# Loading the first rows of wq in four interleaved sets, from two issuing queues

## The chip, the cores and the metric

The kernel runs on one core of a Trainium2 chip. The metric is the device time of one execution in microseconds (us), the median of several runs. A profile of one execution comes with it; its span, from the first to the last instruction, is about 2 us shorter than the device time.

The engines are named as the profile names them: PE (TensorE; PEld is its weight load), DVE (VectorE), ACT (ScalarE), POOL (GpSimd) and SP (SyncE, which here only issues loads). SP and ACT can both issue loads; "SPq" and "ACTq" in the profile are their issuing instructions. The loads themselves are carried out by 16 DMA engines.

## What is computed

One decode step: of the output's rows there is a single one (batch 1, sequence 1, D = 640). It is a block of attention over a sliding window of 4096 cached keys, with 32 heads of 192 columns, and a gated MLP, each behind a layer norm and with a residual:

```python
def _A_ref(x, k_cache, v_cache, wq, wo):
    B, Sq, D = x.shape                       # 1, 1, 640
    Hq, Dh = (32, 192)
    W = min(4096, max(256, Sk // 4))         # 4096 of 32768 cached rows
    q = (x @ wq).reshape(B, Sq, Hq, Dh)      # wq: 640 x 6144, bf16
    k = k_cache[:, :, Sk - W:, :]
    v = v_cache[:, :, Sk - W:, :]
    scores = einsum('bhqd,bhkd->bhqk', q, k) * Dh ** (-0.5)
    o = einsum('bhqk,bhkd->bhqd', softmax(scores), v)
    return o.reshape(B, Sq, Hq * Dh) @ wo    # wo: 6144 x 640
...
x = A_x
h = x + _A_ref(_layernorm(x), A_k_cache, A_v_cache, A_wq, A_wo)
h2 = h + _B_ref(_layernorm(h), B_w_in, B_w_sp, B_b_sp, B_w_out)
```

The keys and the values of the window are 50 MB each, wq and wo 7.9 MB each, w_in and w_out together 3 MB: about 119 MB in all, each byte of it used once.

## The kernel before

A helper records a load on SP's queue. The views of the tensors in memory decide which rows make one contiguous run:

```python
def load(out, in_):
    eng = nc.sync
    eng.add_instruction(mybir.InstDMACopy(
        name=nc.get_next_instruction_name(), mode="Copy", queue="qSPDynamicHW",
        ins=eng.lower_ap_dma(in_, for_custom_bir_dma=True),
        outs=eng.lower_ap_dma(out, for_custom_bir_dma=True)))
...
wq_v = A_wq.rearrange("(c p i) n -> c p (i n)", c=DC, i=4)
...
kvp = ctx.enter_context(tc.tile_pool(name="kv", bufs=KVB))      # KVB = 6
```

wq has five chunks (DC = 5) of 128 rows of 6144 elements. `wq_v[c]` shows a chunk as 32 runs of four rows each (49,152 bytes), which go to 128 partitions, a row to each. Two chunks share a buffer of the kv pool, which wq, the keys and the values use in turn:

```python
def dma_wq(i):
    t = kvp.tile([P, KVE], BF16, tag="kv", name="wq_t")
    for c in range(2 * i, min(2 * i + 2, DC)):
        load(t[:, (c % 2) * HD:(c % 2 + 1) * HD], wq_v[c])
    tiles[("wq", i)] = t
...
plan = [("kv", lambda i=i: dma_wq(i)) for i in range(NWQ)]      # wq first: three buffers
for t_ in range(2):
    plan.append(("kv", lambda t=t_: dma_pair("k", A_k_cache, t)))
...                                                             # then k and v tiles of 3 MB in turn, wo, w_in, w_out
```

Loads are issued as far ahead as buffers are free: at the start that is all of wq and three tiles of keys. Everything else comes after the first call of `issue()`, in this order:

```python
issue()
warm = const.tile([P, 1], F32)
nc.vector.memset(warm[:], 0.0)
nc.scalar.activation(out=warm[:], in_=warm[:], func=ACT.Exp)
nc.scalar.dma_start(out=x_row[:], in_=A_x[0])
...                                       # two more small loads by ACT, constants on DVE and POOL
xc_ps = bank()                            # L241: x to a column form on PE, then the layer norm -> xn2
...
for gq in range(0, NQ, 4):                # the projection to q: 6 sums of 10 matmuls
    for w0 in range(0, 2 * Dh, P):
        psv = sc_bank()[:].rearrange("p (q w) -> p q w", q=4)
        for c in range(DC):
            wc = wq_sb[c // 2][:, (c % 2) * HD:(c % 2 + 1) * HD].rearrange("p (q a w) -> p q a w", q=NQ, a=2)
            for a in range(2):
                nc.tensor.matmul(psv, lhsT=xn2[:, c, a, :], rhs=wc[:, gq:gq + 4, a, w0:w0 + P],     # L264
                                 start=(c == 0 and a == 0), stop=(c == DC - 1 and a == 1))
        nc.scalar.activation(out=q2f[:, gq:gq + 4, w0:w0 + P], in_=psv, func=ACT.Copy, scale=scale / 16)
free("kv", NWQ)                           # the three wq buffers go to v and k tiles
```

Each of the six sums runs over all five chunks. There are two buffers of PSUM for them. After the projection DVE multiplies each tile of keys by its rows of q (L316), PE and others sum the products, and the values and wo follow tile by tile. The last loads are the second half of the last rows of wo (L478 uses them), w_in and w_out for the MLP.

Of the kernel before, what the change touches and what calls it, by code (L numbers as in the profile page):

```python
# [16 lines left out]
def kernel(  # L17
# [14 lines left out]
    nc = tc.nc  # L32
# [6 lines left out]
    DC = D // P  # L39
    HD = H * Dh  # L40
# [12 lines left out]

    NE16 = 32

    def load(out, in_):
        eng = nc.sync
        eng.add_instruction(mybir.InstDMACopy(  # L58
            name=nc.get_next_instruction_name(), mode="Copy", queue="qSPDynamicHW",
            ins=eng.lower_ap_dma(in_, for_custom_bir_dma=True),  # L60
            outs=eng.lower_ap_dma(out, for_custom_bir_dma=True)))

# [8 lines left out]
    win_v = B_w_in.rearrange("(c p) f -> p c f", p=P)  # L71
    wout_v = B_w_out.rearrange("(c e i) n -> c e (i n)", c=FHC, e=NE16)
    wq_v = A_wq.rearrange("(c p i) n -> c p (i n)", c=DC, i=4)
    LAST = (0, J // 2, 3 * J // 4, 7 * J // 8, J)

    KVB = 6
# [13 lines left out]
    def bank():  # L90
        return psum.tile([P, 512], F32, tag="sm", name="sm_ps", bufs=3)
# [9 lines left out]
    def dma_wq(i):  # L101
        t = kvp.tile([P, KVE], BF16, tag="kv", name="wq_t")
        for c in range(2 * i, min(2 * i + 2, DC)):
            load(t[:, (c % 2) * HD:(c % 2 + 1) * HD], wq_v[c])
        tiles[("wq", i)] = t

    def dma_pair(kind, cache, t_):
        t = kvp.tile([P, KVE], BF16, tag="kv", name=kind + "_t")
        cuts = (0, J) if t_ < NP - 1 else LAST if kind == "v" else (0, J // 2, J)
        for a, b in zip(cuts, cuts[1:]):  # L110
            load(t[:, None, a * Dh:b * Dh], pair_keys(cache, t_, a, b))
        tiles[(kind, t_)] = t

    def dma_wo(q):
        t = wop.tile([P, RQ * D], BF16, tag="wo", name="wo_t")
        if q < NQ - 1:
            load(t[:], wo_v[q])
        else:
            rows_v = A_wo.rearrange("(q p i) n -> q p (i n)", q=NQ, p=P)[q]
            for a in range(0, RQ, RQ // 2):  # L120
                load(t[:, a * D:(a + RQ // 2) * D], rows_v[:, a * D:(a + RQ // 2) * D])
        tiles[("wo", q)] = t

    plan = [("kv", lambda i=i: dma_wq(i)) for i in range(NWQ)]
    for t_ in range(2):
        plan.append(("kv", lambda t=t_: dma_pair("k", A_k_cache, t)))
# [269 lines left out]
    def values(t, vt, lo, hi):  # L396
        E = E_bufs[t % NE]
        pv = pv_tiles[t % 2]
        if t == NP - 1:
            for j in range(lo, hi):  # L400
                p0 = 32 * (j % 4)
                nc.tensor.matmul(pv[p0:p0 + 2, 0:Dh], lhsT=E[:, j, :], rhs=vt[:, j * Dh:(j + 1) * Dh],
                                 start=(j < 4), stop=(j >= J - 4))
            return
        v4 = vt[:].rearrange("p (j r i) -> p j r i", r=32, i=RQ)
        for j in range(lo, hi, 8):
            g = j // 8
            for p0, j0, n, i0 in ((0, j, 4, 0), (32, j + 4, 4, 0), (64 + 32 * (g % 2), j, 8, 4)):
                ni = 16 // n
                first = j == 0 if n == 4 else g < 2  # L410
                last = j == J - 8 if n == 4 else g >= J // 8 - 2
                nc.tensor.matmul(pv[p0:p0 + 2 * n, :].rearrange("p (k r i) -> p k r i", k=n, r=32),  # L412
                                 lhsT=E[:, j0:j0 + n, :].rearrange("p j a -> p (j a)"),
                                 rhs=v4[:, j0:j0 + n, :, i0:i0 + ni], start=first, stop=last)

    def scaled(t):
        q, b = divmod(t, 2)
        if b == 0:
            obq[q] = small.tile([P, RQ, 2, 2, 32], BF16, tag="ob", name="ob", bufs=2)
        ob = obq[q][:, :, 0, b, :]  # L420
        pv = pv_tiles[t % 2]
        if t == NP - 1:
            pv1 = pv[:, 0:Dh].rearrange("p (r i) -> p i r", i=RQ)
            R2 = RQ // 2
            for k_ in range(2):
                o_last.append(small.tile([P, R2, 32], BF16, tag=f"ol{k_}", name=f"ol{k_}", bufs=1))
            nc.vector.tensor_copy(out=o_last[0][:], in_=pv1[:, 0:R2])
            nc.scalar.copy(out=o_last[1][:], in_=pv1[:, R2:])
            return
        o1 = small.tile([P, 8, 64], F32, tag="o1", name="o1", bufs=1)  # L430
        nc.vector.tensor_tensor(out=o1[:], in0=pv[:].rearrange("p (k w) -> p k w", k=8),
                                in1=m8[:, :, None].to_broadcast([P, 8, 64]), op=ALU.mult)
        flat = o1[:].rearrange("p k w -> p (k w)")
        for n, i0 in ((4, 0), (8, 4)):
            ni = 16 // n
            with nc.allow_low_precision(reason="one nonzero term"):
                nc.vector.tensor_reduce(out=ob[:, i0:i0 + ni], in_=flat.rearrange("p (k r i) -> p i r k", k=n, i=ni),  # L437
                                        axis=AX.X, op=ALU.add)

    def columns(oT, q, b):  # L440
        for i in range(RQ):
            lhsT = obq[q][:, i, 0, 0, :] if b == 0 else o_last[i // 3][:, i % 3, :]
            s_ = sel[i // 4] if b == 0 else sel_1
            for a in range(2):
                p0 = 64 * a + 32 * b
                nc.tensor.matmul(oT[p0:p0 + 32, i:i + 1], lhsT=lhsT, rhs=s_[:, a:a + 1], start=True, stop=True)
# [36 lines left out]
    def fold(rows_sb):  # L483
        n = CUT[1] // P
        for c in range(n):
            w = 2 if c + n < DC else 1
            nc.tensor.matmul(attn_ps[:, c:c + n * (w - 1) + 1:n], lhsT=rows_sb[:, c * P:(c + 1) * P], rhs=halfsel[:, 0:w],
                             start=(c == 0), stop=False)
# [71 lines left out]
    vt = tiles.pop(("v", NP - 1))  # L560
    values(NP - 1, vt, 0, LAST[-3])
    fold(rows_sb)
    values(NP - 1, vt, LAST[-3], LAST[-2])
    oT = bank()
    columns(oT, NQ - 1, 0)
    values(NP - 1, vt, LAST[-2], J)
    scaled(NP - 1)
# [90 lines left out]
```

## Time and profile before

| what | value |
|---|---|
| device time, median of 3 runs | 286.56 us (286.56 to 286.75) |
| span of the profiled execution | 284.7 us |
| busiest engine | DVE, 218.4 us |
| bytes on SP's load queue | 119.35 MB |
| wq loads | 5 of 1536 KB each, median 11.2 us from issue to landing |
| first wq issue by SP; issue of x_row by ACT | 0.74 us; 0.91 us |
| first and last start of a projection matmul | 9.8 us; 34.9 us |

How to read such a profile: the busy shares say which engine works most, but not which of them sets the end. For that one looks at the stages one by one, at the load queues beside the engines, and at the chain of waits that ended last, followed back from the last instruction. The records of the DMA packets, from which the loads' share comes, give the start, length and size of every single transfer on the 16 DMA engines. Times in the views are in us from the start of the span; "L264" is a line of the kernel.

### The profile page before, as it was taken

What the parts mean: (1) busy time and instruction counts of PE and PEld (TensorE: products, weight loads), DVE (VectorE), ACT (ScalarE), POOL (GpSimd) and SP (SyncE); (2) the same over time, 40 slices, a digit from 0 to 9 for tenths busy, and PEclk for the clock granted to TensorE, in tenths of its full rate; (3) what the DMA queues carried; (4) which work ended last, traced back from release to release, by engine and by line L of the source; (5) the groups of instructions that cost most, each with busy time, mean ns of one, the idle gap of its engine ahead of it and who ended that gap; (6) DMA issues with size and microseconds to landing.
All of it is one profiled execution on the core that took longest, in us unless ns stands there. A gap on an engine that the chain in (4) does not pass through costs nothing.

```text
span 284.7 us, 3101 instructions
## 1 busy us (share of the span) xinstructions
PE 167.1 (59%) x1110; PEld 65.3 (23%) x1110; DVE 218.4 (77%) x288; ACT 75.2 (26%) x380; POOL 2.3 (1%) x10
## 2 busy tenths in 40 slices
PE   0329935773755377725852585536971767764774
PEld 0103412221211022211220121112320222321463
DVE  7300099889999999998499999996699949995443
ACT  2001247413274431122344440143101010202301
POOL 3000000000000000000000000000000000000000
PEclk9999979796598557955799558955797797999785
DMA  8999999999998999999999999999999999999993
GB/s 332 435 435 408 435 429 402 444 463 435 435 435 382 435 442 443 427 464 424 414 442 421 443 428 439 407 457 428 410 435 456 442 442 383 435 435 425 401 406 141
DMA packets 5404, 119.53 MB, mean 420 GB/s; under 512 B 973, under 2 KB 2254, under 8 KB 2830
## 3 DMA queue, kind: packets, MB, share of 16 engines
q1 hardware_dynamic: 5384, 119.35, 97.8%
q8 instruction: 8, 0.13, 0.2%
q14 instruction: 6, 0.05, 0.0%
q10 hardware_dynamic: 6, 0.00, 0.0%
HBM read 119.34 MB, written 0.00 MB: 419 GB/s over the span
## 4 chain that ended last, share of the span: by engine, by line
DMA 42%; DVE 41%; PE 13%; issue 2%; SPq 1%; ACT 0%; DVEq 0%; ACTq 0%
DVE k_t L316 22%; DMA k_t<-in_A_k_cache_dram 21%; DMA v_t<-in_A_v_cache_dram 9%; DMA wq_t<-in_A_wq_dram 7%; DMA wo_t<-in_A_wo_dram 5%; PE sc_ps L264 5%; DVE S L309 5%; DVE ob L437 4%; DVE S L330 4%; PE sc_ps L323 3%; PE pv_174 L412 1%; PE attn_ps L473 1%; SPq L58 1%; PE sm_ps L340 1%; DVE gm L342 1%
## 5 line engine op out<-in xcount | busy, mean ns | idle before, releaser
L316 DVE TENSOR_TENSOR k_t<-k_t,q_205 128x6144 bf16<-128x6144 bf16 x32 | 107.1, 3351 | 13.1 <-DMA k_t<-in_A_k_cache_dram 13.1
L323 PE MATMUL sc_ps<-k_t,ident_bf 128*128 128x512 bf16 x282 | 87.1, 468 | 50.6 <-DVE k_t L316 50.6
L306 ACT ACTIVATE k_t<-k_t 128x192 bf16<-128x192 bf16 x144 | 49.9, 347 | 32.8 <-DVE k_t L316 32.8
L323 PEld LDWEIGHTS <-ident_bf 128*128 128x128 bf16 x282 | 30.6, 113 | 98.3 <-issue 63.9
L306 ACT ACTIVATION_READ_ACCUMULATOR k_t<-k_t 128x1 f32 x144 | 26.8, 186 | 0.0
L309 DVE TENSOR_REDUCE S<-k_t 128x16 f32<-128x3072 bf16 x8 | 26.8, 3345 | 0.0
L264 PE MATMUL sc_ps<-wq_t,xn_126 128*128 128x512 bf16 x60 | 17.4, 449 | 10.4 <-DMA wq_t<-in_A_wq_dram 8.1
L330 DVE TENSOR_REDUCE S<-sc_ps 128x16 f32<-128x512 f32 (+1 forms) x32 | 21.8, 682 | 0.5 <-PE sc_ps L323 0.5
L273 DVE TENSOR_SCALAR sp_f<-sm_ps 128x1 f32<-128x1 f32 x3 | 0.3, 153 | 25.3 <-PE sm_ps L270 25.3
L359 ACT ACTIVATE E_125<-S,bias 128x64 bf16<-128x64 f32 x10 | 3.5, 360 | 48.1 <-DVE bias L349 48.1
L359 ACT ACTIVATE E_123<-S,bias 128x64 bf16<-128x64 f32 x12 | 4.2, 360 | 41.9 <-DVE bias L349 41.9
L359 ACT ACTIVATE E_124<-S,bias 128x64 bf16<-128x64 f32 x10 | 3.5, 361 | 37.9 <-DVE bias L349 37.9
L266 ACT ACTIVATE q_205<-sc_ps 128x512 bf16<-128x512 f32 x6 | 3.6, 597 | 30.1 <-PE sc_ps L264 30.1
L264 PEld LDWEIGHTS <-xn_126 128*128 128x128 bf16 x60 | 6.5, 109 | 20.9 <-issue 13.6
L412 PE MATMUL pv_174<-v_t,E_124 128*8 128x512 bf16 (+1 forms) x72 | 8.9, 521 | 2.0 <-DMA v_t<-in_A_v_cache_dram 2.0
L342 DVE TENSOR_REDUCE gm<-sm_ps 2x1 f32<-2x128 f32 x16 | 4.5, 278 | 7.1 <-PE sm_ps L340 7.1
L412 PE MATMUL pv_172<-v_t,E_125 128*8 128x512 bf16 (+1 forms) x72 | 7.5, 472 | 3.1 <-DMA v_t<-in_A_v_cache_dram 3.1
L412 PE MATMUL pv_174<-v_t,E_123 128*8 128x512 bf16 (+1 forms) x48 | 5.8, 521 | 1.0 <-DMA v_t<-in_A_v_cache_dram 1.0
L412 PE MATMUL pv_172<-v_t,E_123 128*8 128x512 bf16 (+1 forms) x72 | 6.2, 424 | 0.0
L412 PE MATMUL pv_174<-v_t,E_125 128*8 128x512 bf16 (+1 forms) x48 | 5.0, 474 | 1.6 <-DMA v_t<-in_A_v_cache_dram 1.6
L412 PEld LDWEIGHTS <-E_125 128*8 128x8 bf16 (+1 forms) x120 | 3.5, 87 | 9.3 <-issue 7.2
L412 PEld LDWEIGHTS <-E_124 128*8 128x8 bf16 (+1 forms) x120 | 3.6, 89 | 8.3 <-issue 6.4
(237 smaller groups left out, 148.3 us busy)
## 6 DMA issues: line engine op xcount, KB each, us to landing
k_t<-in_A_k_cache_dram SPq DMA_DIRECT2D x15, 3072.0 KB, 29.8
v_t<-in_A_v_cache_dram SPq DMA_DIRECT2D x15, 3072.0 KB, 29.6
wq_t<-in_A_wq_dram SPq DMA_DIRECT2D x5, 1536.0 KB, 11.2
wo_t<-in_A_wo_dram SPq DMA_DIRECT2D x7, 960.0 KB, 19.9
k_t<-in_A_k_cache_dram SPq DMA_DIRECT2D x2, 1536.0 KB
v_t<-in_A_v_cache_dram SPq DMA_DIRECT2D x1, 1536.0 KB
w_in_sb<-in_B_w_in_dram SPq DMA_DIRECT2D x2, 576.0 KB, 14.6
wo_t<-in_A_wo_dram SPq DMA_DIRECT2D x2, 480.0 KB, 13.8
```

What stands on the lines that cost most here:

```text
L58: eng.add_instruction(mybir.InstDMACopy(name=nc.get_next_instruction_name(), mode="Copy", queue="qSPDynamicHW", ins=eng.lower_ap_dma(in_, ...
L264: nc.tensor.matmul(psv, lhsT=xn2[:, c, a, :], rhs=wc[:, gq:gq + 4, a, w0:w0 + P], start=(c == 0 and a == 0), stop=(c == DC - 1 and a == 1))
L266: nc.scalar.activation(out=q2f[:, gq:gq + 4, w0:w0 + P], in_=psv, func=ACT.Copy, scale=scale / 16)
L306: nc.scalar.activation(out=k3[:, j, :], in_=k3[:, j, :], func=ACT.Copy, accum_out=S[:, j:j + 1])
L309: nc.vector.tensor_reduce(out=st[t]["S"][:, J - JS:J], in_=products(t)[:, J - JS:J, :], axis=AX.X, op=ALU.add)
L316: nc.vector.tensor_tensor(out=kc, in0=kc, in1=q2[:, t:t + 1, :].to_broadcast([P, JC, Dh]), op=ALU.mult)
L323: nc.tensor.matmul(psv, lhsT=ident_bf[:], rhs=products(t)[:, j0:j1, n * g:(n + 1) * g], start=(n == 0), stop=(n == Dh // g - 1))
L330: nc.vector.tensor_reduce(out=S[:, j0:j1], in_=st[t]["ps"][ch], axis=AX.X, op=ALU.add)
L342: nc.vector.tensor_reduce(out=gm[:], in_=mT[0:2, 0:P], axis=AX.X, op=ALU.max)
L359: nc.scalar.activation(out=E[:, :, a], in_=S[:], func=ACT.Exp, bias=bias[:, a:a + 1], accum_out=zq[q][:, a, b:b + 1])
L412: nc.tensor.matmul(pv[p0:p0 + 2 * n, :].rearrange("p (k r i) -> p k r i", k=n, r=32), lhsT=E[:, j0:j0 + n, :].rearrange("p j a -> p (j a)" ...
L437: nc.vector.tensor_reduce(out=ob[:, i0:i0 + ni], in_=flat.rearrange("p (k r i) -> p i r k", k=n, i=ni), axis=AX.X, op=ALU.add)
```

## The change

The change cuts the loads of the first four wq chunks into sets of interleaved rows: four sets of every fourth row for chunks 0 and 1, two sets of every second row for chunks 2 and 3. Chunk 4 stays as it was. A row is now a run of its own (12,288 bytes). Of chunk 0, sets 1 and 3 are issued from ACT's queue and sets 0 and 2 from SP's, so that two queues have work at the start. Its purpose is to have the first rows under way sooner: each of the first loads is smaller and two of them can be issued at the same time. The same bytes go to the same partitions as before, and nothing else in the program is changed.

```diff
-    def load(out, in_):
-        eng = nc.sync
+    def load(out, in_, eng=nc.sync):
         eng.add_instruction(mybir.InstDMACopy(
-            name=nc.get_next_instruction_name(), mode="Copy", queue="qSPDynamicHW",
+            name=nc.get_next_instruction_name(), mode="Copy", queue="qSPDynamicHW" if eng is nc.sync else "qActDynamicHW",
             ins=eng.lower_ap_dma(in_, for_custom_bir_dma=True),
             outs=eng.lower_ap_dma(out, for_custom_bir_dma=True)))
...
     wq_v = A_wq.rearrange("(c p i) n -> c p (i n)", c=DC, i=4)
+    wq_rows = A_wq.rearrange("(c p) n -> c p n", c=DC)
+    WQ_PARTS = (4, 4, 2, 2, 1)
...
         for c in range(2 * i, min(2 * i + 2, DC)):
-            load(t[:, (c % 2) * HD:(c % 2 + 1) * HD], wq_v[c])
+            n = WQ_PARTS[c]
+            for j in range(n):
+                dst = t[j::n, (c % 2) * HD:(c % 2 + 1) * HD]
+                load(dst, wq_rows[c, j::n] if n > 1 else wq_v[c], nc.scalar if c == 0 and j % 2 else nc.sync)
         tiles[("wq", i)] = t
```

In the call of `issue()` the two loads on ACT's queue stand ahead of the activation that warms up ACT and of the load of x_row.

## The prediction

> **What bounds the kernel now.** I read the page's shares first, then the load by stage, then the start of the timeline, then the waits, the chain of waits and the packet records of the trace.
>
> ```profile
> span 284.7 us, 3101 instructions
> PE 167.1 (59%) x1110; PEld 65.3 (23%) x1110; DVE 218.4 (77%) x288; ACT 75.2 (26%) x380; POOL 2.3 (1%) x10
> ...
> q1 hardware_dynamic: 5384, 119.35, 97.8%
> ```
>
> The busiest engine, DVE, works 77% of the span; the SP load queue (q1) keeps the 16 DMA engines busy for 97.8%. The table by stage says where the other 2.2% are (columns: stretch, length, busy us of each engine, clock, DMA share, GB/s):
>
> ```profile
> 0.00:2.00 2.00, 0.00 (x0) 0.00 (x0) 0.77 (x6) 1.27 (x1) 1.33 (x10) 1.00 0.00 1
> 2.00:22.00 20.00, 5.00 (x16) 1.78 (x17) 6.75 (x48) 0.22 (x2) 0.95 (x1) 1.00 1.03 433
> 22.00:100.00 78.00, 49.38 (x225) 18.10 (x224) 61.38 (x56) 32.38 (x167) 0.00 (x0) 0.83 1.00 432
> 100.00:180.00 80.00, 47.95 (x283) 16.56 (x284) 71.76 (x73) 24.33 (x134) 0.00 (x0) 0.72 1.00 431
> 180.00:260.00 80.00, 49.60 (x311) 18.74 (x311) 67.02 (x75) 11.78 (x60) 0.00 (x0) 0.83 1.00 432
> ...
> 281.00:285.00 4.00, 0.70 (x24) 0.43 (x12) 0.32 (x1) 0.00 (x0) 0.00 (x0) 0.50 0.00 0
> ```
>
> Nothing moves for 2 us, then 431 to 433 GB/s without a hole until the end, then a tail of nearly 4 us without loads. The packet records agree: data run from 2.07 to 280.95 us, and a packet of 49,152 B takes 1.815 us, so 16 engines give 16 x 49,152 / 1.815 us = 433 GB/s. The run is one long load stream with a fixed head and tail. Its end reaches the output through the last wo rows, as the chain of waits says:
>
> ```profile
> 260.22 13.82 DMA wo_t<-in_A_wo_dram
> 274.08 0.54 PE attn_ps L478 x15
> ```
>
> From 274.08 to 284.7 us there are 10.6 us of short dependent steps that the change doesn't touch. So a change in the start of the stream, or in its total work, moves the end by as much; a change of any engine's work in the first 35 us moves nothing unless it starves the stream.
>
> The place that the change touches is this (start, us, what; in brackets the idle time before):
>
> ```profile
> 0.74 3.15 SPq L58 DMA_DIRECT2D wq_t<-in_A_wq_dram  x5
> ...
> 0.91 0.50 ACTq L155 DMA_DIRECT2D x_row<-in_A_x_dram  x1
> ...
> 9.76 1.03 PE L264 MATMUL sc_ps<-wq_t,xn_126 128*128 128x512 bf16 x2 [2.25 <-DVE xn_126 L251]
> ...
> 11.03 1.01 PE L264 MATMUL sc_ps<-wq_t,xn_126 128*128 128x512 bf16 x2 [0.24 <-DMA wq_t<-in_A_wq_dram]
> ...
> 21.95 4.27 PE L264 MATMUL sc_ps<-wq_t,xn_126 128*128 128x512 bf16 x10 [2.60 <-DMA wq_t<-in_A_wq_dram]
> ```
>
> Five issues take 0.55 to 0.63 us each while one chunk of wq (1.57 MB) takes 3.63 us to move, so issuing is far ahead of moving. The first matmuls wait for xn2, not for the first rows. The fifth chunk lands at 21.95, and only then do 52 of the 60 matmuls run (13.3 us): earlier first rows let TensorE begin earlier and wait longer. Even this projection's end is not the bound: the v tile that follows it is issued at 34.02, with the third k tile still moving until about 2.4 + 17.3 MB / 433 GB/s = 42 us.
>
> [...]
>
> **The change part by part.**
>
> *Work of the stream.* Packets are as long as the source's contiguous run. A chunk before is 32 runs of four rows (49,152 B), two per engine. In chunks 0 to 3 a run becomes one row of 12,288 B, eight per engine. The kernel before has 64 packets of that size, for a part of the last v tile: 0.460 us each. One chunk goes from 2 x 1.815 = 3.63 to 8 x 0.460 = 3.68 us, plus some 3 ns between packets: +0.07 us. Four chunks: **+0.27 us**. Chunk 4 keeps its form. Loads go from 5 to 13, and each ends with a small record that costs an engine about 15 ns: 8 x 15 = **+0.12 us**. Sum +0.39 us, on every engine, all on the path.
>
> *Start of the stream.* Before, ten engines begin their first packet at 2.07 to 2.16 us, the other six at 2.32 to 2.90, and these first packets take 2.06 to 2.68 us in place of 1.815. The slowest engine begins at 2.66 and ends at 5.23, as if it had begun at full speed at 3.41. The engines that began early end from 4.45 on, as if begun at 2.64 to 3.03. All engines move the same bytes, so the lag of the last lasts: the ends of first packets are 0.8 us apart, and the ends of the last data at 280 us too. Two first issues side by side[...] should let the late six begin nearer to the others. If the slowest then does as the early ones did, the gain is 3.41 - 3.03 = 0.4 to 3.41 - 2.64 = 0.8 us. How far it goes I can't read from a trace; I choose **-0.55 us**. The first packet itself can hardly come earlier: the four-row store at the end, far smaller, also takes 1.23 us from issue to first packet (282.10 to 283.33), against 1.33 for wq.
>
> *Issue.* SP issues 11 parts, 11 x 0.6 = 6.6 us in place of 3.15; a part of 0.39 MB keeps the engines busy for 0.92 us, more than its 0.6 us of issue. No hole from that.
>
> *x_row.* Its load stands behind two issues of ACT (1.1 us) [...] I expect it near 6.2 in place of 2.2 us. VectorE takes its result at 6.49 before, after its constants, so xn2 comes 0 to 1 us later, and TensorE begins at 10 to 11 us. The last chunk at about 22 hides all of it: **0**.
>
> Sum: 0.39 - 0.55 = -0.16 us, so 286.56 - 0.16 = **286.4 us**.
>
> **The rivals.**
>
> *A. The start doesn't change* (the late engines are late for another reason, or two issuers at once get in each other's way). Then only the extra packets stay: +0.39, or 286.95 us; with some clash of the two queues up to 287.3. For it: the spread of 0.8 us is of one run, and its cause isn't in the profile.
>
> *B. The head is cut by more.* If all engines start at 2.1 us and the slow first packets shrink as well, up to 1.1 us is gained, 0.7 net: 285.85 us. Against it: the slow first packets look like a price of the first access, which small packets pay too.
>
> *C. A new wait on the load queue.* The program has eight completion semaphores for these loads; the ninth waits until the first has landed:
>
> ```profile
> SPq L58 <- DMA wq_t<-in_A_wq_dram: 5.2, 2, 3.5
> ```
>
> The first k tile is that ninth one; the timeline has its issue at 7.36, when the first wq chunk was in:
>
> ```profile
> 7.36 1.90 SPq L58 DMA_DIRECT2D k_t<-in_A_k_cache_dram  x3
> ```
>
> With 13 parts and three small ACT loads the wq loads themselves come to wait. Eight in flight less three small ones is five parts of 0.92 us, 4.6 us of queued work, against 1.3 us from an issue to its first packet. So these waits should lie beside a busy stream. If a slot hangs on x_row's late landing, a hole of 1 to 2 us could open: 288 us. I give that 5%.
>
> *D. TensorE's earlier start shortens the run.* It would need the projection to be the bound; the 21.95 us line speaks against it. Worth 0.
>
> **Range and chances.** A and B span 285.85 to 286.95; a little more each way for the clash of queues and for the tail gives **285.7 to 287.3**. Two per cent is 5.7 us, more than the whole head of the stream, so faster 0.01, within 2% 0.97, slower 0.02.
>
> **What would show it.** The loads' share stays near 98%, and the rate from 2 to 260 us stays at 431 to 433 GB/s. The wq packets of 12,288 B take 0.46 us each, 32 per engine. The engines' first packets begin within about 0.4 us of each other (if still within 0.8, A). The fifth chunk's matmuls begin at 21.6 to 22.1, and the last wo rows' at 273.7 to 274.2. The x_row matmuls begin near 6 us, and that moves nothing. It would be wrong if the table by stage showed a stretch before 45 us under 420 GB/s (C), or if the tail after the wo rows were no longer 10.6 us.

## The result, and the profile after

| | before | changed |
|---|---|---|
| device time, median | 286.71 us (286.56 to 286.8) | 289.44 us (288.51 to 290.55) |
| ratio, 95% interval | | 1.0098 [1.0071, 1.0124] |
| span of the profiled execution | 284.7 us | 288.5 us |
| fifth chunk's matmuls begin | 21.95 us | 23.84 us |
| last data of the last load | 280.95 us | 283.04 us |

The change costs 2.7 us. The prediction was 286.4 us in a range of 285.7 to 287.3: it is outside. In the changed kernel the lines below the change stand 4 lower (L264 is L268, L478 is L482).

The page of the changed kernel, its shares and its load queues; q10 is ACT's queue, with the two sets of chunk 0:

```profile
span 288.5 us, 3115 instructions
PE 173.5 (60%) x1110; PEld 67.5 (23%) x1110; DVE 218.5 (76%) x288; ACT 75.2 (26%) x380; POOL 2.3 (1%) x10
...
q1 hardware_dynamic: 5800, 118.56, 96.3%
q10 hardware_dynamic: 102, 0.79, 0.6%
```

DVE does the same work (218.5 us; 218.4 before) and the two queues move the same 119.35 MB, so no work was added. The stages of the changed kernel (stretch, length, busy us of PE, PEld, DVE, ACT, POOL, clock, DMA share, GB/s) say where the time went:

```profile
2.00:22.00 20.00, 4.84 (x15) 1.57 (x16) 6.89 (x48) 1.49 (x2) 0.95 (x1) 1.00 1.02 393
22.00:45.00 23.00, 16.33 (x59) 6.31 (x58) 7.02 (x7) 6.50 (x23) 0.00 (x0) 0.95 1.00 434
...
100.00:180.00 80.00, 48.47 (x271) 15.99 (x269) 73.66 (x73) 26.67 (x147) 0.00 (x0) 0.72 1.00 431
180.00:260.00 80.00, 51.98 (x304) 19.32 (x303) 67.03 (x72) 11.01 (x56) 0.00 (x0) 0.79 1.00 432
...
270.00:281.00 11.00, 9.91 (x186) 7.37 (x174) 4.99 (x15) 0.98 (x4) 0.00 (x0) 0.50 1.02 399
```

From 22 to 260 us the rate is as before (431 to 434 GB/s); the end is looked at below. From 2 to 22 us the stream gives 393 in place of 433 GB/s: 20 us x 40 GB/s = 0.8 MB, or 1.85 us of stream, and the fifth chunk is 1.89 us late. The DMA share of that stretch, 1.02 (1.03 before), shows nothing of it: the engines count as busy and move less. Shorter stretches of the same table, where the packets are those of the sets:

```profile
4.00:7.00 3.00, 0.00 (x0) 0.00 (x0) 2.42 (x24) 0.00 (x0) 0.00 (x0) 1.00 1.02 430
7.00:11.00 4.00, 0.88 (x7) 0.70 (x7) 1.77 (x10) 0.00 (x0) 0.00 (x0) 1.00 0.99 366
...
12.00:17.50 5.50, 2.31 (x6) 0.38 (x4) 0.00 (x0) 0.00 (x0) 0.00 (x0) 1.00 0.95 331
```

There are two slow stretches. In the packet records the 512 packets of 12,288 B take 0.517 us on average, where 0.460 was expected. In the slow stretches the median is still 0.460 us, but about a fifth of the packets take more than 0.6 us, single ones up to 2.1 us.

The timeline of the changed kernel (start, busy us, what; in brackets the idle time before, and what ended it):

```profile
0.73 10.87 SPq L57 DMA_DIRECT2D wq_t<-in_A_wq_dram  x11
0.74 1.47 ACTq L57 DMA_DIRECT2D wq_t<-in_A_wq_dram  x2
2.31 0.77 ACTq L159 DMA_DIRECT2D x_row<-in_A_x_dram  x1
...
7.86 0.28 PE L245 MATMUL sm_ps<-ones_bf,x_row 1*128 1x1 bf16 x5 [7.86 <-DMA x_row<-in_A_x_dram]
...
11.45 1.89 PE L268 MATMUL sc_ps<-wq_t,xn_134 128*128 128x512 bf16 x4 [2.26 <-DVE xn_134 L255]
11.64 2.07 SPq L57 DMA_DIRECT2D k_t<-in_A_k_cache_dram  x3
...
16.53 1.03 PE L268 MATMUL sc_ps<-wq_t,xn_134 128*128 128x512 bf16 x2 [3.19 <-DMA wq_t<-in_A_wq_dram]
20.23 1.03 PE L268 MATMUL sc_ps<-wq_t,xn_134 128*128 128x512 bf16 x2 [2.67 <-DMA wq_t<-in_A_wq_dram]
23.84 8.45 PE L268 MATMUL sc_ps<-wq_t,xn_134 128*128 128x512 bf16 x27 [2.57 <-DMA wq_t<-in_A_wq_dram]
```

The 11 issues of SP take 10.87 us and not 6.6: some of them wait for a completion slot, one of eight, which a load holds until its data have landed: in the kernel before, eight loads were issued by 3.27 us without such a wait, and the ninth at 7.36 us. The waits of SP's queue in the changed kernel name what for (us in total, times, longest):

```profile
SPq L57 <- DMA wq_t<-in_A_wq_dram: 4.2, 3, 2.8
```

The slots were taken in a fixed turn, in which ACT's small loads counted like any other. The kernel before shows it:

```profile
2.21 0.28 PE L241 MATMUL sm_ps<-ones_bf,x_row 1*128 1x1 bf16 x5 [2.21 <-DMA x_row<-in_A_x_dram]
```

Here x_row had landed by 2.21 us and its slot was free, and still the ninth load waited until 7.36 us for the first wq chunk. In the changed kernel the first eight loads are five sets and three small ones, so already the sixth set has to wait for a landing.

The trace has the start of every issue. From the bytes issued and the bytes moved by then one gets the work still pending at that time (at 433 GB/s; a dash means that its slot was free by then; some issues are left out):

| SP's issue in the changed kernel | starts at | released by | pending before it |
|---|---|---|---|
| first five sets (SP's and ACT's) | 0.74 to 1.97 us | nothing | up to 3.63 us |
| chunk 1, second set | 5.43 us | landing of ACT's first set | 2.01 us |
| chunk 1, third set | 5.94 us | – | 2.42 us |
| chunk 1, fourth set | 7.83 us | landing of ACT's second set | 1.59 us |
| chunk 2, first set | 8.35 us | – | 2.11 us |
| chunk 3, first set | 9.63 us | – | 4.60 us |
| first k tile | 11.64 us | – | 10.06 us |

There was work pending at every one of these issues. But the queue was short, and it was slow: that is the reading to be tested. The theory is that the eight completion slots leave too little work queued, and that packets lengthen then (called "slots" below, S in the expectations). Its rivals: the two queues get in each other's way (Q); the shorter packets cost more than worked out (P); the form of the sets (every second or fourth row) keeps the engines from their full rate (R).

### The profile page after: what moved, and what is told of

Read it like the earlier page. It is cut to its first block, busy times and chain, and to the rows that moved or that the text cites. A ratio compares the mean times of both kernels' runs of the same rounds, so it can differ in the third digit from the quotient of the medians.

```text
span 288.5 us, 3115 instructions
## 1 busy us (share of the span) xinstructions
PE 173.5 (60%) x1110; PEld 67.5 (23%) x1110; DVE 218.5 (76%) x288; ACT 75.2 (26%) x380; POOL 2.3 (1%) x10
## 4 chain that ended last, share of the span: by engine, by line
DVE 37%; DMA 36%; PE 21%; issue 3%; SPq 1%; ACT 0%; ACTq 0%; DVEq 0%
DMA k_t<-in_A_k_cache_dram 20%; DVE k_t L320 19%; DMA v_t<-in_A_v_cache_dram 9%; PE sc_ps L327 7%; DMA wq_t<-in_A_wq_dram 7%; PE sc_ps L268 5%; DVE ob L441 5%; DVE S L313 3%; DVE S L334 3%; PE attn_ps L477 2%; PE pv_182 L416 2%; SPq L57 1%; PE sm_ps L344 1%; PE pv_182 L406 1%; DVE gm L346 1%
## 5 line engine op out<-in xcount | busy, mean ns | idle before, releaser
L327 PE MATMUL sc_ps<-k_t,ident_bf 128*128 128x512 bf16 x282 | 89.5, 478 | 47.1 <-DVE k_t L320 47.0
L327 PEld LDWEIGHTS <-ident_bf 128*128 128x128 bf16 x282 | 31.2, 116 | 96.8 <-issue 66.6
L268 PE MATMUL sc_ps<-wq_t,xn_134 128*128 128x512 bf16 x60 | 17.8, 461 | 10.7 <-DMA wq_t<-in_A_wq_dram 8.4
L334 DVE TENSOR_REDUCE S<-sc_ps 128x16 f32<-128x512 f32 (+1 forms) x32 | 21.9, 683 | 1.7 <-PE sc_ps L327 1.7
L268 PEld LDWEIGHTS <-xn_134 128*128 128x128 bf16 x60 | 6.4, 110 | 21.7 <-DMA wq_t<-in_A_wq_dram 7.7
L416 PE MATMUL pv_182<-v_t,E_132 128*8 128x512 bf16 (+1 forms) x72 | 8.8, 511 | 2.1 <-DMA v_t<-in_A_v_cache_dram 2.1
L416 PE MATMUL pv_180<-v_t,E_133 128*8 128x512 bf16 (+1 forms) x72 | 7.1, 457 | 1.7 <-DMA v_t<-in_A_v_cache_dram 1.7
L416 PE MATMUL pv_182<-v_t,E_131 128*8 128x512 bf16 (+1 forms) x48 | 6.7, 569 | 1.1 <-DMA v_t<-in_A_v_cache_dram 1.1
L416 PE MATMUL pv_180<-v_t,E_131 128*8 128x512 bf16 (+1 forms) x72 | 7.1, 457 | 0.0
L416 PE MATMUL pv_182<-v_t,E_133 128*8 128x512 bf16 (+1 forms) x48 | 5.0, 472 | 0.5 <-DMA v_t<-in_A_v_cache_dram 0.5
```

The costliest lines, as they stand in the source:

```text
L327: nc.tensor.matmul(psv, lhsT=ident_bf[:], rhs=products(t)[:, j0:j1, n * g:(n + 1) * g], start=(n == 0), stop=(n == Dh // g - 1))
L334: nc.vector.tensor_reduce(out=S[:, j0:j1], in_=st[t]["ps"][ch], axis=AX.X, op=ALU.add)
```

## The experiments

Times are medians beside runs of the kernel before on the same chip (286.68 or 286.76 us). "Lowest pending" is the least work pending at an issue of a wq load by SP after 4 us (at the first k tile where no wq load waits). The ratio is estimated from all runs and is not quite that of the two medians: for r9 the medians are 2.5 us apart, and the ratio stands for 1.9.

| run | us | ratio, 95% | fifth chunk at | last data at | lowest pending |
|---|---|---|---|---|---|
| kernel before | 286.7 | | 21.95 | 280.95 | 13.7 |
| r1 the change again | 289.61 | 1.0098 [1.0082, 1.0115] | 24.59 | 283.91 | 1.45 |
| r2 one load per chunk, packets of a row | 286.89 | 1.0008 [0.9996, 1.0021] | 22.29 | 281.31 | 13.7 |
| r3 all sets from SP | 288.18 | 1.0052 [1.0035, 1.0068] | 23.00 | 282.25 | 2.95 |
| r4 sets in chunk 0 alone | 286.91 | 1.0002 [0.9989, 1.0014] | 22.06 | 281.05 | 4.73 |
| r5 x_row first, two small loads later | 287.34 | 1.0021 [1.0010, 1.0032] | 22.46 | 281.48 | 5.2 |
| r6 two sets per chunk, SP | 287.34 | 1.0018 [1.0007, 1.0029] | 22.12 | 281.39 | 6.5 |
| r7 four sets in chunk 3 alone, SP | 287.24 | 1.0022 [1.0012, 1.0033] | 22.45 | 281.43 | 8.1 |
| r8 as r7, sets of adjacent rows | 292.23 | 1.0182 [1.0163, 1.0201] | 27.16 | 286.11 | – |
| r9 sets in chunks 0 and 1 | 289.21 | 1.0067 [1.0042, 1.0092] | 23.54 | 282.89 | 2.59 |
| r10 two small loads later | 287.20 | 1.0015 [0.9994, 1.0036] | 22.07 | 281.20 | 3.88 |
| r11 as r5, sets in chunk 0 alone | 287.18 | 1.0023 [1.0006, 1.0040] | 22.27 | 281.26 | 13.5 |
| r12 kernel before and 0.79 MB more | 288.53 | 1.0058 [1.0039, 1.0078] | 23.91 | 282.89 | – |

**r1: the change again**, unaltered.

> The changed kernel unaltered, as the measure for the others. If the loss sits at the head of the load stream, the fifth chunk's matmuls start at 23.5 to 24.2 us again (21.95 before), and the dips in the load rate near 7 to 11 and 12 to 17 us come back; the time is 288.5 to 290.5. If the dips were an accident of one execution, that start moves by over 1 us and the time with it.

Two of its stages, and where the fifth chunk comes in:

```profile
7.00:11.00 4.00, 0.89 (x7) 0.70 (x7) 1.70 (x10) 0.00 (x0) 0.00 (x0) 1.00 0.97 341
...
12.00:17.50 5.50, 1.93 (x6) 0.27 (x5) 0.00 (x0) 0.00 (x0) 0.00 (x0) 1.00 0.97 351
```

```profile
24.59 1.86 PE L268 MATMUL sc_ps<-wq_t,xn 128*128 128x512 bf16 x4 [2.60 <-DMA wq_t<-in_A_wq_dram]
```

The same two slow stretches at the same places: they belong to the program and are no accident of one execution. The fifth chunk comes 0.4 us later than the expectation allowed; this execution was 0.3 us behind the first one already at 6 us.

**r2: the packets without the sets.** One load per chunk, all from SP, chunks 0 to 3 in packets of a row.

```diff
-WQ_PARTS = (4, 4, 2, 2, 1)
+WQ_PARTS = (1, 1, 1, 1, 1)
...
-load(dst, wq_rows[c, j::n] if n > 1 else wq_v[c], nc.scalar if c == 0 and j % 2 else nc.sync)
+load(dst, wq_rows[c, j::n] if c < 4 else wq_v[c], nc.scalar if c == 0 and j % 2 else nc.sync)
```

> Chunks 0 to 3 in rows of 12,288 bytes as in the change, but one load for each chunk, all from SP: only the packet size is changed. Theory S (eight completion slots: small loads wait for slots, the load queue runs shallow, and packets with nothing behind them take longer): no shallow queue, packets 0.46 us each, fifth chunk's matmuls at 22.2 to 22.5, time 286.8 to 287.3. Theory P (short row packets are slow by themselves): packets of 0.5 us and more, 23.5 to 24, time 289. Theory Q (two issuing queues get in each other's way): as before, 21.9 to 22.5.

```profile
7.00:11.00 4.00, 1.53 (x4) 0.68 (x5) 2.21 (x9) 0.00 (x0) 0.00 (x0) 1.00 1.02 433
...
12.00:17.50 5.50, 1.35 (x3) 0.25 (x2) 0.00 (x0) 0.00 (x0) 0.00 (x0) 1.00 1.04 442
```

No slow stretch. The packets take 0.460 us once the first ones are through, the fifth chunk comes 0.34 us later than before, and the time is 0.13 us up, with an interval of the ratio that holds 1. The shorter packets are not the cause.

**r3: one issuing queue.** All 13 sets from SP.

```diff
-load(dst, wq_rows[c, j::n] if n > 1 else wq_v[c], nc.scalar if c == 0 and j % 2 else nc.sync)
+load(dst, wq_rows[c, j::n] if n > 1 else wq_v[c], nc.sync)
```

> All 13 sets of the change, but all from SP's queue, none from ACT. Theory S: the same 16 loads share the same eight slots, so the loss stays: fifth chunk's matmuls at 23.3 to 24.2, time 288.3 to 290. Theory P: the same. Theory Q: the loss goes, 22.0 to 22.4 and 286.7 to 287.2.

```profile
4.00:7.00 3.00, 0.10 (x1) 0.10 (x1) 2.61 (x26) 0.00 (x0) 0.00 (x0) 1.00 0.95 320
```

Half of the loss stays, a little less than expected (23.00 us for 23.3 to 24.2). x_row now lands at 2.19 us, and the slow stretch lies earlier, from 4 to 7 us; the rates after it are nearer to full. A second queue is not needed for the loss (1.05 us at the fifth chunk), but with it the loss is larger (1.89 us, and 2.64 in r1).

**r4: sets in chunk 0 alone**, from both queues as in the change.

```diff
-WQ_PARTS = (4, 4, 2, 2, 1)
+WQ_PARTS = (4, 1, 1, 1, 1)
```

> Only chunk 0 in four sets, two from ACT and two from SP; the other chunks in one load each as before. Theory S: large loads stand behind the small ones, the queue stays deep; fifth chunk's matmuls at 21.7 to 22.3, time 286.3 to 287. Theory Q: both queues clash as in the change, 23 to 24, time 288 to 289. Theory P: a quarter of the loss, 22.4, time 287.2.

The timeline of r4, projection and x_row:

```profile
12.24 0.29 PE L245 MATMUL sm_ps<-ones_bf,x_row 1*128 1x1 bf16 x5 [12.24 <-DMA x_row<-in_A_x_dram]
...
15.83 3.59 PE L268 MATMUL sc_ps<-wq_t,xn 128*128 128x512 bf16 x8 [2.25 <-DVE xn L255]
22.06 10.20 PE L268 MATMUL sc_ps<-wq_t,xn 128*128 128x512 bf16 x35 [2.63 <-DMA wq_t<-in_A_wq_dram]
```

Two queues, sets of every fourth row and three small loads behind ACT's sets: all of it is there, and nothing is lost. Behind the sets stand whole chunks, so that there is always work (4.73 us at the least). It shows too that x_row came ten microseconds late (12.24 for 2.2 us) and TensorE began at 15.83 us, at no cost (286.91 us). And it says that the start of the stream gains nothing from two small first loads: the first packets still take 0.56 us per engine too long (0.57 before).

**r5 and r6: free slots, fewer sets.** r5 is the change with x_row loaded ahead of `issue()` and the two other small loads of ACT (2 bytes each) moved behind the projection. r6 has two sets in each of the chunks 0 to 3, all from SP.

```diff
+nc.scalar.dma_start(out=x_row[:], in_=A_x[0])                          # r5, ahead of issue()
...
-nc.scalar.dma_start(out=wsp_bf[:, 0:1], in_=B_w_sp[0:1])               # r5, moved
-nc.scalar.dma_start(out=wsp_bf[:, 1:2], in_=B_b_sp.rearrange("(o n) -> o n", o=1))
...
 free("kv", NWQ)
+nc.scalar.dma_start(out=wsp_bf[:, 0:1], in_=B_w_sp[0:1])               # r5, to here
+nc.scalar.dma_start(out=wsp_bf[:, 1:2], in_=B_b_sp.rearrange("(o n) -> o n", o=1))
```

```diff
-WQ_PARTS = (4, 4, 2, 2, 1)
+WQ_PARTS = (2, 2, 2, 2, 1)                                             # r6, and every load from nc.sync
```

> The change with ACT's x_row load ahead of its two wq sets, and its two other small loads put off until after the projection: two queues and 13 sets as in the change, but in the first microseconds no small load holds one of the eight slots behind ACT's sets. Theory S (SP's sets wait for slots, one of them for a late load of ACT): the wait of SP up to 7.8 us shortens and the dip at 7 to 11 us goes; fifth chunk's matmuls at 22.3 to 23, time 287 to 288. Theory Q (two queues clash): no better than the change, 23.8 to 24.6 and 289. Theory R (sets of every second or fourth row make the DMA engines disturb each other): the dip at 12 to 17 us stays, 23 to 24.

> Chunks 0 to 3 in two sets of every second row each, all from SP: loads twice as large as the small ones, so over 5 us of work stand queued at every issue. Theory S: no dip after the first microseconds, fifth chunk's matmuls at 22.2 to 22.6, time 286.8 to 287.3. Theory R: packets of 0.5 us and more all through the four chunks, 23 to 24, time 288 to 289.

Both end at 287.34 us, with more than 5 us of work pending throughout. r5 has all 13 sets and both queues, and shows no slow stretch (418, 421 and 425 GB/s from 4 to 7, 7 to 11 and 12 to 17.5 us). Both are still 0.66 us slower than the kernel before by the medians, with intervals clear of 1; that rest is not explained.

**r7 and r8: the form of the sets, in a deep queue.** Chunk 3 alone in four sets, behind three whole chunks. r7 keeps every fourth row; r8 takes 32 adjacent rows into 32 adjacent partitions.

```diff
-WQ_PARTS = (4, 4, 2, 2, 1)
+WQ_PARTS = (1, 1, 1, 4, 1)                                             # r7 and r8, all from nc.sync
...
-dst = t[j::n, (c % 2) * HD:(c % 2 + 1) * HD]                           # r8
+R = P // n
+dst = t[j * R:(j + 1) * R, (c % 2) * HD:(c % 2 + 1) * HD]
...
-load(dst, wq_rows[c, j::n] if n > 1 else wq_v[c], ...)
+load(dst, wq_rows[c, j * R:(j + 1) * R] if n > 1 else wq_v[c], nc.sync)
```

> Only chunk 3 in four sets of every fourth row, all from SP, behind three whole chunks: small sets in a deep queue. Theory S: the sets' packets take 0.46 us, fifth chunk's matmuls at 21.9 to 22.2, time as before. Theory R: they take 0.5 to 0.6, 22.3 to 23.

> As the run with chunk 3 in four sets behind three whole chunks, but each set is 32 adjacent rows in place of every fourth, so that it goes to 32 adjacent partitions. [...] the packets take about twice as long, 0.8 to 0.95 us, chunk 3 takes 7 us in place of 3.7 and the fifth chunk's matmuls start at 25 to 26; if partitions don't matter, 21.9 to 22.2.

r7 moves its sets at 0.468 us a packet: with at least 8.1 us of work pending, the interleaved sets ran at nearly the full rate (0.460 us). Its fifth chunk is later than "slots" had it (22.45 us for 21.9 to 22.2), but 0.38 us of these 0.50 were lost before the sets: the second chunk's matmuls began at 11.41 us (11.03 before). r8 doesn't run at that rate; the timeline of r8 at chunks 3 and 4:

```profile
23.90 1.04 PE L269 MATMUL sc_ps<-wq_t,xn 128*128 128x512 bf16 x2 [6.91 <-DMA wq_t<-in_A_wq_dram]
27.16 5.28 PE L269 MATMUL sc_ps<-wq_t,xn 128*128 128x512 bf16 x12 [2.22 <-DMA wq_t<-in_A_wq_dram]
```

Its packets take 0.888 us on average: 16 x 12,288 B / 0.888 us = 221 GB/s, half the rate. The loss, 5.2 us at the fifth chunk, is larger than I had expected (25 to 26 us for it); the 16 whole-chunk packets behind the sets are slow too, 2.2 to 3.2 us in place of 1.815. Why this form costs half the rate is not shown. Sets of every fourth row did not pay it (0.468 us in r7).

**r9: whole chunks behind the sets.** Sets in chunks 0 and 1 only.

```diff
-WQ_PARTS = (4, 4, 2, 2, 1)
+WQ_PARTS = (4, 4, 1, 1, 1)
```

> The change, but chunks 2 and 3 in one load each, as before: the same first eight sets from two queues, the same shallow start, no sets of every second row behind it. Theory S [...]: the dip at 7 to 11 us stays, the one at 12 to 17 us goes; fifth chunk's matmuls at 22.5 to 23.3, time 287.2 to 288. If the second dip comes from issuing or from the wait for slots alone, it stays: 23.8 to 24.6, time 289 or more.

It missed: 289.21 us where I had expected 287.2 to 288. The first slow stretch is still there and lasts longer (327 to 394 GB/s in the single microseconds from 7 to 14 us, each packet's bytes spread over its length), beside a short queue (2.59 us). From 14 us on the rate is full (429 GB/s in the table from 12 to 17.5 us), but the first four whole-chunk packets after the sets take 2.9 to 3.2 us in place of 1.815, so most of the loss of the second stretch comes in another form.

**r10: two slots freed, and nothing else.** The change with the two loads of 2 bytes moved behind the projection (the last edit of r5). x_row stays behind ACT's sets.

```diff
-nc.scalar.dma_start(out=wsp_bf[:, 0:1], in_=B_w_sp[0:1])
-nc.scalar.dma_start(out=wsp_bf[:, 1:2], in_=B_b_sp.rearrange("(o n) -> o n", o=1))
...
 free("kv", NWQ)
+nc.scalar.dma_start(out=wsp_bf[:, 0:1], in_=B_w_sp[0:1])
+nc.scalar.dma_start(out=wsp_bf[:, 1:2], in_=B_b_sp.rearrange("(o n) -> o n", o=1))
```

> The change with nothing else altered than that ACT's two 2-byte loads are put off until after the projection, so that two of the eight slots are free for wq sets at the start; x_row stays behind the sets. Theory S: two more sets are issued without a wait, the work pending at SP's issues stays over 3 us; fifth chunk's matmuls at 22.2 to 22.9, time 286.9 to 287.6. If slots don't matter: 23.8 to 24.6 and 289 to 289.7, as the change.

The stages of r10, its timeline, and the wait of SP's queue:

```profile
7.00:11.00 4.00, 0.89 (x7) 0.71 (x7) 1.55 (x9) 0.00 (x0) 0.00 (x0) 1.00 1.01 427
...
12.00:17.50 5.50, 2.71 (x6) 0.46 (x5) 0.11 (x1) 0.00 (x0) 0.00 (x0) 1.00 1.02 431
```

```profile
8.18 0.28 PE L243 MATMUL sm_ps<-ones_bf,x_row 1*128 1x1 bf16 x5 [8.18 <-DMA x_row<-in_A_x_dram]
...
22.07 10.23 PE L266 MATMUL sc_ps<-wq_t,xn 128*128 128x512 bf16 x38 [2.56 <-DMA wq_t<-in_A_wq_dram]
```

```profile
SPq L57 <- DMA wq_t<-in_A_wq_dram: 7.0, 4, 3.1
```

Moving 4 bytes of loads brings back 2.2 to 2.4 us of the 2.7 to 2.85; at the fifth chunk it is a little more than expected (22.07 us for 22.2 to 22.9). The second and third sets of chunk 1 are issued at 2.61 and 3.31 us, not at 5.43 and 5.94; SP still waits for the same landings afterwards, at 5.57 and 7.91 us, but with 3.88 and 4.29 us pending in place of 2.01 and 1.59. Both slow stretches are gone (427 and 431 GB/s). The 7.0 us of waits are not to be laid beside the 4.2 of the changed kernel, since they contain waits of k tiles: up to 12 us SP waits for 2.6 us here and for 4.0 there. A wait with much work pending cost nothing here: beside the one of 3.5 us in the kernel before, with 13.7 us pending, the stream ran at 433 GB/s. The two small loads themselves are not to blame: their data take an engine 9 ns each, and in r4 they stood in the same place and did no harm.

**r11: the start once more.** r5's moves with sets in chunk 0 alone.

> What the change was for with its costs taken away: only chunk 0 in four sets from two queues, the x_row load ahead of them, ACT's two 2-byte loads put off. If a quicker start is to be had, fifth chunk's matmuls at 21.4 to 21.7 and 286.1 to 286.4; if the first packets' delay is a fixed price per engine, 21.9 to 22.2 and 286.6 to 287.

No quicker start here either, and the time is above both expectations (287.18 us). Counted in bytes, r11 is at 6 us as far as if it had run at 433 GB/s from 3.19 us on. For the kernel before this is 2.91 us, for the changed one 2.92, and for the other runs 2.98 to 3.22 (without r3, which by then is in its slow stretch). No size of the first packets and no number of issuing queues gave an earlier start than before. The price isn't the same in every execution: the change gave 2.92 once and 3.19 in r1.

**r12: what a shift of the head is worth.** The kernel before with one more load of 0.79 MB ahead of chunk 4, which nothing reads.

```diff
+if c == DC - 1:
+    load(t[:, HD:HD + HD // 2], A_wq[0:P, 0:HD // 2])
 load(t[:, (c % 2) * HD:(c % 2 + 1) * HD], wq_v[c])
```

> The kernel before, with half a chunk of wq (0.79 MB, 1.82 us at 433 GB/s) read once more into an unused half of a buffer, ahead of the fifth chunk: the load stream shifted by a known time, no sets, one queue. If what the change lost at the head passes to the end one for one, the fifth chunk's matmuls come at 23.7 to 23.9 and the time is 288.4 to 288.8; if a shift of the head costs more at the end than itself (the change shows 2.7 us for 1.9), 289 to 289.6; if it is absorbed, under 288.

A piece of r12's chain of waits, to be laid beside the same piece of the kernel before (260.22):

```profile
262.14 13.82 DMA wo_t<-in_A_wo_dram
```

The fifth chunk comes 1.96 us later, the last rows of wo 1.92 us later, the time is 1.85 us up. What the head lost here, the end lost, nearly one for one.

## Why the prediction was wrong

**What bounds the kernel: right.** The stream from 2 us on sets the time; r12 shows that a shift of its head is passed on (1.96 us at the fifth chunk, 1.85 us in the time).

**The step that failed** is the estimate behind rival C, that the waits for completion slots "should lie beside a busy stream", with "five parts of 0.92 us, 4.6 us of queued work". Two things were wrong in it. First the size: five sets are 4.6 us of work when they have just been issued, and not when the next one may be. The queue had 2.01, 2.42, 1.59 and 2.11 us left at the issues from 5.43 to 8.35 us, because three of the eight turns were those of small loads, and the next sets in turn had to wait for ACT's two sets. These were worked off in turn with SP's and had landed only at 5.4 and 7.8 us. The late x_row, which C feared for, held up no set: when its slot came up, at 9.63 us, it had landed. Secondly the criterion: I looked for a hole, where nothing is queued, and compared with 1.3 us from issue to first packet. There was no hole of that kind. From 4 to 22 us the packet records give 1.46 us per engine in longer packets and 0.35 us without a packet (at 12.7 us 6 of the 16 engines had none). So most of the loss is engines that were busy and slow. Sorted by the lowest pending work, the runs with sets of every fourth or second row show it: 1.45 to 2.95 us (r1, r9, r3) cost 2.85, 2.5 and 1.4 us; 3.88 us and more (r10, r4, r5, r6, r7, r11) cost 0.15 to 0.66 us. r10 moves this quantity with almost nothing else and is the ground for calling the slots the cause. That pending work is the measure, and where its limit lies, rests on this sorting alone. The chance of 5% for C was too low, but the place it named, a stretch before 45 us under 420 GB/s, is the one where the loss lies.

**The work of the stream: too large, if anything.** I had +0.27 us for shorter packets. r2 is 0.34 us late at the fifth chunk, but 0.31 us of it are its later start (3.22 for 2.91 us); from 6 to 20 us, which holds most of the row packets, it loses only 0.06 us more than the kernel before. The +0.12 us for more loads is too small to be seen apart.

**The start: wrong.** The gain of 0.55 us doesn't exist. The first packets of the changed kernel begin from 2.10 us on (2.07 before), and at 6 us it is as far as the kernel before (2.92 and 2.91 us, counted as under r11); r4 and r11 are no earlier. This is rival A, and without the slots it would have given 286.95 us; r4, r10 and r11 are at 286.9 to 287.2.

**x_row and TensorE: late, and harmless as said.** x_row landed at 7.86, not near 6.2 us, which was an estimate of mine. The trace has the 32 packets of SP's first set, two for each engine, and then ACT's 32 from 3.49 us on, though ACT's issue was only 5 ns after SP's: the queues took turns here by sets, not by packets of the trace. How much of the delay this explains is not worked out. r4 is the proof of the harmlessness (12.24 us, and 286.91 us in all).

**The tail: not longer, but reached on another path.** The 10.6 us were counted from 274.08 us, the second half of the matmuls with the last wo rows, which waited for their load. The first half had begun earlier:

```profile
273.26 0.51 PE L478 MATMUL attn_ps<-o_1888,wo_t 128*128 128x1 bf16 x15 [0.32 <-DVE o_1888 L464]
274.08 0.53 PE L478 MATMUL attn_ps<-o_1888,wo_t 128*128 128x1 bf16 x15 [0.30 <-DMA wo_t<-in_A_wo_dram]
```

In the changed kernel all 30 run in one piece and wait for VectorE, not for the load, as the chain of waits says:

```profile
276.93 0.23 DVE o_1896 L468
277.21 0.95 PE attn_ps L482 x30
```

From the first of the 30 to the end it is 11.4 us before (from 273.26) and 11.3 us after. What came late is the path before it: the stream was 1.85 us behind at 260 us, but the span is 3.8 us longer. TensorE's granted clock was 0.50 from 270 to 281 us (0.73 before), and 5.5 us passed after the last data (3.8 before). That this belongs to the execution rather than to the change is supported by r4, whose profiled execution took 288.22 us where its median is 286.91: clock 0.50 again, 5.5 us after the last data, and the same chain:

```profile
274.89 0.23 DVE o L468
275.17 0.95 PE attn_ps L482 x30
```

So the head accounts for about 1.9 us of the first profiled execution (2.2 us in r1); how the rest of the 2.7 us in the median comes about, over executions without a profile, is not shown.

**What stays open.** Why packets lengthen with little queued, no view shows. Nor is it explained why the stretch from 12 to 17.5 us is slow, when 10 us of work are pending again, and why r9's first one goes on until 14 us, with 9 us pending from 8.7 us on: r10 shows that the second stretch goes with the first, and r9 that it changes form with what is queued behind. So little pending work (1.45 to 2.95 us) started a slow stretch in these runs, and much of it (9 to 10 us) did not end one at once. No run changed the number of slots itself; r10 frees turns in them. The traces don't name a packet's engine.

No version beat the kernel before. The best, r2, r4 and r10, are the same as it within their intervals.

## What to carry to other kernels

Before a load is split, count the completion slots and everything that takes a turn in them, the smallest loads too: here a load of 2 bytes took a turn like one of 1.5 MB, and two of them cost 2.2 to 2.4 us (r10). Judge a load queue by the microseconds of work pending at each issue and by its GB/s, not by its share of busy time (1.02 here, at 393 GB/s) or the length of the issuer's waits (3.5 us in the kernel before, at 433 GB/s). In this kernel, bound by one long stream, the fifth chunk gates the work: first projection matmuls at 15.83 in place of 9.76 us cost nothing (r4), while 1.96 us lost in the head were 1.85 us of the time (r12). Before a profiled execution is read for its end, compare its time with the median: r4's was 1.3 us above its own, with a clock of 0.50 at the end.

## What the runs showed of the hardware

- In the changed kernel, with 1.59 to 2.4 us of work pending at the issues from 5.43 to 8.35 us, packets of 12,288 B took 0.517 us on average and single ones up to 2.1 us, at a DMA share of 0.95 to 1.02 in the stretches shown. In r2, with 13.7 us pending at the first wait, the average was 0.481 us, and 0.460 once the first packets were through.
- The eight completion slots went by turn in the kernel before: a landed x_row (2.21 us) did not let the ninth load go before the first wq chunk was in (7.36 us).
- The first packets of the 14 profiled executions took 0.32 to 0.75 us per engine longer than later ones, for packets of 49,152 B (0.32 to 0.67) as of 12,288 B (0.32 to 0.75).
- In the changed kernel two sets issued 5 ns apart from two queues were fetched set by set in turn, two of the trace's packets per engine, the second set from 3.49 us on.
- The same bytes in sets of 32 adjacent rows and partitions ran at 0.888 us a packet (221 GB/s), in sets of every fourth at 0.468 us, 16 x 12,288 B / 0.468 us = 420 GB/s.
